# A Mixture-of-Experts and S4 kernel: skip term moved, first two groups re-dealt, S4 paced by single operations

## The chip, the cores and the metric

The kernel runs on one core of one Trainium2 chip. A core has TensorE (PE, matrix products; PEld is its weight load), VectorE (DVE), ScalarE (ACT), GpSimd (POOL) and SyncE (SP), which run their own instruction queues in order and wait for one another by semaphores. SP and POOL issue the DMAs here; those of POOL can add to what lies at their destination. The metric is the time of one execution in microseconds, less is better; several runs are timed, and one execution is recorded by the hardware profiler.

## The reference

One input `u` of 2048 tokens by 512 channels is normalised per token, and the output is the input plus two branches of the normalised `xn`:

```
xn = layernorm(x)
# branch A: S4 convolution, per channel d, along the 2048 tokens
K  = real(sum_n C[d,n] * dt[d] * B[d,n] * exp(dt[d] * A[d,n] * l))
yA = causal_convolution(K, xn) + xn * Dskip
# branch B: 8 experts, all kept (top 8 of 8), so each token goes through each expert
gates = softmax(xn @ w_gate)
yB = sum_e gates[:, e] * (silu(xn @ w1[e]) @ w2[e])        # 512 -> 1792 -> 512
out = x + yA + yB
```

All of it is in 32-bit floats on the outside.

## The kernel before

**Products in halves.** Each operand is split into two 16-bit floats, a high and a low part, and a product is made of three matmuls (high by high, high by low, low by high). ACT makes the high part (a scaled copy), DVE the low part (a scaled subtraction). The scales are powers of two from sums of squares over a weight tensor: ACT squares (`square`, `first_square`), PE totals over the partitions (`pow2_total`), DVE turns the total into an exponent (`pow2_exponent`, `pow2`).

**Tiles.** Tokens go in 4 groups ("token blocks", `tb`) of 512, each 4 tiles of 128. The hidden width 1792 goes in 7 pairs of 256 (`NPR`), taken two at a time by `DQS = [(0, 1), (2, 3), (4, 5), (6,)]`; so a group has four blocks `d`, the last of half the size. The outer order is expert `e`, group `tb`, block `d`; 8 x 4 groups in all.

**A block** (`block`) has four steps, called slots; 16 slots make a group. It uses seven products instead of eight for the first weight (a Strassen-like scheme on sums of operands: `x_sums` makes the seven operands of the tokens, `w1_sums` those of the weights). Products land in three PSUM tiles A, B and C (`hb`), ACT copies A to B and B to C (lines 1337 and after), keeps copies in SBUF (`keep`), POOL adds two of these by DMA, and `activate` applies SiLU and the high split on ACT; the low split follows on DVE later (`flush`). Its result is put on the list `units`. `pop(n)` takes n units off that list and multiplies each with the second weight into one of four PSUM tiles y: six matmuls of 512 columns. When a tile y has all its 14 units, `evacuate` reads it out on ACT to a tile "ye" and a DMA adds it to the DRAM sum `oacc`. The tiles ye and the skip tiles share one tag, "stg", of four buffers.

**The first group** (`plain`, expert 0, group 0) uses ordinary products, because the seven-product operands aren't there yet. It has 14 slots, one per half pair. In its slots the other preparations happen: squares of the second weight, splits of the first (`plain_split`), and the operands of group 1, which `x_turn` transposes through a PSUM bank on PE. That one bank ("s4") is used in turn by transposes, gate products, totals and S4; `take_bank` hands it on, and who takes it first reads out what the last user left.

**The order is written by hand.** The program is emitted in the order in which each engine shall run it. Dictionaries `early`, `mid` and `side` say what is emitted in which slot, before a slot's product, after it, and after its units (`at(n, f)` puts f in slot n of expert 0, counted 16 per group; `put` takes expert, group, block and slot). `slot` runs them, then `work_on(limit)` lets up to `limit` steps of the next expert's weight work through (list `work`: squares, totals, splits), if they are ready.

**S4** runs behind the products: `background` is a generator that is asked for its next piece while a budget lasts. `bg_run` gives it a share of planned PE time less what DVE was given otherwise; each piece says what it costs (`tt_`, the planner's estimate of a DVE operation), and a piece may say that it must wait. S4 goes in 32 chunks of 16 channels: tables (`s4_tables`), kernel generation, transforms on PE, `s4_conv` on DVE, back transform. Every second chunk needs a new basis (`s4_basis`), whose three sine operations on ACT are put on `act_later` and emitted by `run_later`, in the third slot of the two middle blocks. All S4 must be emitted before the last group: `bg_until("s4")` emits the rest there.

**The skip term** `u + xn * Dskip` of token tile i is loaded by `base(i)` on SP, computed by `base_add(i)` on DVE, and added to `oacc` by `base_send(i)` on POOL, in slots 4 to 13 of expert 1's first three groups and expert 2's first.

Of the kernel before, what the change touches and what calls it, by code (L numbers as in the profile page):

```python
# [32 lines left out]
def s4_moe_kernel(  # L33
# [64 lines left out]
    clock = {"slot": 0, "pe": 0.0, "pe0": 0.0, "dve": 0.0, "dve0": 0.0, "left": 0.0}  # L98
# [147 lines left out]
    def x_high(g, a):  # L246
        hi = xs_["hi"] = sb.tile([P, 7, TH], F16, tag="ta", name=f"xh{g}_{a}", bufs=1)
        for src, n0, n in xs_["f"]:
            S.copy(hi[:, n0:n0 + n, :].rearrange("p o d -> p (o d)"), src.rearrange("p o d -> p (o d)"))

# [7 lines left out]
    def x_turn(g, a, q):  # L258
# [17 lines left out]
        else:  # L276
            xs = sb.tile([P, 8, P], F16, tag="hh", name=f"xs{g}_{a}_{q}", bufs=9)
            S.copy(xs[:, :n, :], tp[:, :n, :])
            bank["at"] = now()
# [5 lines left out]
    def xplain(j, rs8):  # L285
# [4 lines left out]
        hlf = hl.rearrange("p a k t -> p a (k t)")  # L290
        S.copy(hlf[:, 0, :], xn)
        V.tensor_tensor(hlf[:, 1, :], xn, hlf[:, 0, :], op=ALU.subtract)
# [5 lines left out]
    def xplain_out(j):  # L298
        dst = xT0.rearrange("p a k t -> p (a k) t")[:, :, j * P:(j + 1) * P]
        if j % 2:  # L300
            V.tensor_copy(dst, xp[j])
        else:
            S.copy(dst, xp[j])
# [123 lines left out]
    def square(e, w, pr, raw):  # L427
        rf = raw.rearrange("p a c -> p (a c)")
        S.activation(rf, rf, AF.Square, accum_out=rows_of(e, w)[:, pr:pr + 1])

# [56 lines left out]
    def piece_end(e, w, n, ready):  # L487
# [15 lines left out]
        def later():  # L503
            return now() > st["at"] + 1 and bank_free()
# [147 lines left out]
    def s4_tables(c):  # L652
# [6 lines left out]
        for st in range(6):  # L659
# [19 lines left out]
            yield 3 * tt_(2 * nn * L) + 0.3 * (st == 0)  # L679
# [69 lines left out]
    def s4_conv(c):  # L749
# [14 lines left out]
        for m in range(NI):  # L764
# [11 lines left out]
            if m in (1, 3, 5, 7, 9, 12, 15):  # L776
# [24 lines left out]

    def tt_(n):

        return n / 960 + 0.14
# [178 lines left out]
    xplain(0, rs8_0)  # L983
    V.tensor_reduce(row2[:, 0:1], rows_of(0, 0)[:, 0:2], axis=AX.X, op=ALU.add)
    keep_busy(8, ident)
    stA = pow2_total(row2[:, 0:1], 1, "a")
    take_bank()
    xplain(1, rs8_0)
# [3 lines left out]
    sq(2)  # L992
    xplain_out(0)
    low0 = first_split(0)
    keep_busy(8, ident)
    xplain(2, rs8_0)
    low0()
    sq(3)
    xplain_out(1)
    keep_busy(8, ident)  # L1000
    xplain(3, rs8_0)
    sq(4)
    xplain_out(2)
    low1 = first_split(1)
    xplain_out(3)
    keep_busy(6, ident)
# [28 lines left out]
    def piece_sums(pr):  # L1035
# [12 lines left out]
    work.extend((w_[0], w_[1], s_[0], w_[2], s_[1], w_[3], s_[2], w_[4], s_[3], w_[5], w_[6], s_[4], s_[5], s_[6]))  # L1048
# [22 lines left out]
    SHARE = 0.96  # L1071
# [13 lines left out]

    def bg_until(key):
# [5 lines left out]
    def run_later():  # L1092
        while act_later and act_later[0][0] <= clock["slot"]:
            act_later.pop(0)[1]()
            s4["sines"] = now()
# [24 lines left out]
    def evacuate(e, i, y):  # L1120
        g = gates_e[e][:, i:i + 1]
        if e < E - 1 or i < NT - TPB:
            t = sb.tile([P, D], F32, tag="stg", name=f"ye{e}_{i}", bufs=4)
            S.activation(t, y, AF.Copy, scale=g)  # L1124
            if e:
# [43 lines left out]
    def activate(e, tb, d, src, fh, th, whole=False):  # L1169
# [4 lines left out]
        sc = scales[e]  # L1174
# [6 lines left out]
        S.activation(ahl[:, 0, :n], fa, AF.Copy, scale=sc[:, 3:4])  # L1181

        def low():
            V.scalar_tensor_tensor(ahl[:, 1, :n], fa, sc[:, 3:4], ahl[:, 0, :n], op0=ALU.mult, op1=ALU.subtract)  # L1184
# [28 lines left out]

    def at(n, f, where=side):
        where.setdefault((0, n // 16, n % 16 // 4, n % 4), []).append(f)
    for n in range(7):
        at(n // 2, lambda n=n: first_square(1, n, second[n], n % 2 == 1))
    at(0, first_scales, mid)
    at(0, third)
    for n in range(4):  # L1220
        at(2 * n + 1, lambda n=n: plain_split(3 + n))
# [4 lines left out]
    at(6, gates_split)  # L1226
    at(4, lambda: norm_sums(1))
    at(7, lambda: x_stats(1))
    at(8, lambda: x_sums(1, 0))
    at(8, lambda: x_high(1, 0))  # L1230
    at(9, lambda: x_low(1, 0))
    at(9, lambda: x_sums(1, 1))
    at(9, less)
    for n, (a, q, where) in enumerate(((0, 0, early), (0, 1, mid), (0, 2, early), (0, 3, mid))):
        at(10 + n // 2, lambda q=q: x_turn(1, 0, q), where)
# [230 lines left out]
```

## Time and profile before

| what | value |
|---|---|
| median of 3 runs | 2415.71 us (2413.98 to 2416.49) |
| the profiled execution, its own time | 2415.3 us |
| its span, first to last instruction | 2413.5 us |
| PE busy | 2354.6 us (98%) |
| VectorE busy | 1955.1 us (81%) |
| ScalarE busy | 1426.2 us (59%) |
| GpSimd busy | 339.2 us (14%) |
| mean granted TensorE clock | 0.993 |

Busy time is the union of an engine's instruction spans. A wait row names the engine, what it wanted to write and the line, then the engine and instruction whose end released it, and then the total, the count and the longest in us. A timeline row has the start, the length of the merged stretch, the instruction, and in brackets how long the engine stood before it and for whom. A row of groups has the count, then the busy time and the mean length in ns of one, and the idle time before them. A row of windows has, for each stretch, the busy us of PE, PEld, DVE, ACT and POOL with their counts, the granted clock, and the DMA share.

### The profile page before, as it was taken

To read this page: it belongs to the slowest core of one execution; us is meant where nothing else is said; L and a number is where in the kernel's file an instruction comes from. 1 tells how busy PE (TensorE), PEld (TensorE's weight loads), DVE (VectorE), ACT (ScalarE), POOL (GpSimd) and SP (SyncE) were. 2 spreads that over 40 slices of the span, in tenths; PEclk is the share of its full clock that TensorE was granted. 3 is DMA by queue.
4 is the path that set the end of the run, shared out by engine and by line. 5 is a ranking of instruction groups with operands and counts; after the bars stand their busy time and mean duration, and the time that the engine had idled before them with its cause. 6 is when DMAs were issued, how large, how long until landed. Compare 5 with 4: busy or idle time off the path is not lost.

```text
span 2413.5 us, 44927 instructions
## 1 busy us (share of the span) xinstructions
PE 2354.6 (98%) x17663; PEld 1564.7 (65%) x17663; DVE 1955.1 (81%) x3836; ACT 1426.2 (59%) x2435; POOL 339.2 (14%) x394
## 2 busy tenths in 40 slices
PE   7789999999999999999999999999999999999999
PEld 4466666666666666666666666666666666666665
DVE  7663588689985999998889799999898799999611
ACT  6477575555646657565675566665575655754443
POOL 0000001211121110111110111111111101111112
PEclk9899999999999999999999999999999999999999
DMA  6466366574664645565465554655555644633356
GB/s 223 144 164 192 74 173 150 132 176 86 175 144 112 133 98 163 108 135 117 106 162 118 120 132 99 160 116 123 122 115 140 143 110 105 165 65 72 76 115 149
DMA packets 264644, 314.41 MB, mean 130 GB/s; under 512 B 124464, under 2 KB 158768, under 8 KB 264112
## 3 DMA queue, kind: packets, MB, share of 16 engines
q1 hardware_dynamic: 208560, 217.93, 29.6%
q0 software_dynamic: 55872, 93.61, 24.5%
q8 instruction: 138, 2.26, 0.4%
q14 instruction: 74, 0.61, 0.1%
HBM read 201.09 MB, written 60.82 MB: 109 GB/s over the span
## 4 chain that ended last, share of the span: by engine, by line
PE 82%; issue 7%; ACT 4%; DVE 3%; DMA 1%; POOL 1%; SPq 0%; DVEq 0%; POOLq 0%; ACTq 0%
PE hb L1162 36%; PE y L1146 14%; PE y L1148 14%; PE y L1147 14%; PE kgen L690 1%; ACT w1s L432 1%; PE yp L791 1%; PE kf L742 1%; PE uf L731 1%; PE hb L1384 1%; PE tp L267 1%; DVE w1s L435 1%; ACT fa L1179 0%; DMA oacc<-ye 0%; ACT ahl L1181 0%
## 5 line engine op out<-in xcount | busy, mean ns | idle before, releaser
L1162 PE MATMUL hb<-xop,w1s 128*128 128x256 f16 x9114 | 1074.9, 273 | 9.1 <-ACT scC L1333 6.8
L1162 PEld LDWEIGHTS <-w1s 128*128 128x128 f16 x9114 | 889.9, 98 | 186.9 <-issue 11.7
L1146 PE MATMUL y<-w2s,ahl 128*128 128x512 f16 x1792 | 680.6, 380 | 10.2 <-ACT ye L1124 10.2
L1148 PE MATMUL y<-w2s,ahl 128*128 128x512 f16 x1792 | 680.9, 380 | 0.0
L1147 PE MATMUL y<-w2s,ahl 128*128 128x512 f16 x1792 | 680.8, 380 | 0.0
L1148 PEld LDWEIGHTS <-ahl 128*128 128x128 f16 x1792 | 175.4, 98 | 212.1 <-issue 0.8
L1306 POOL DMA_DIRECT2D scC<-sE x124 | 111.6, 900 | 1363.6 <-ACT sE L1333 880.2
L1147 PEld LDWEIGHTS <-ahl 128*128 128x128 f16 x1792 | 175.4, 98 | 177.4 <-issue 12.3
L1146 PEld LDWEIGHTS <-ahl 128*128 128x128 f16 x1792 | 175.4, 98 | 165.2 <-issue 0.8
L774 DVE TENSOR_TENSOR s<-s,tm 128x720 f32<-128x720 f32 (+14 forms) x480 | 269.0, 560 | 16.6
L773 DVE TENSOR_TENSOR tm<-v,k 128x720 f32<-128x720 f32 (+14 forms) x480 | 267.7, 558 | 10.9
L1184 DVE SCALAR_TENSOR_TENSOR ahl<-fa,sc,ahl 128x512 f16<-128x512 f32 (+1 forms) x262 | 178.8, 683 | 90.1 <-ACT ahl L1181 90.0
L1179 ACT ACTIVATE fa<-hb,sc 128x512 f32<-128x512 f32 (+1 forms) x252 | 160.0, 635 | 149.7 <-PE hb L1162 141.1
L1344 ACT COPY hb<-hb 128x512 f32<-128x512 f32 x124 | 64.1, 517 | 261.6 <-PE hb L1162 261.6
L1181 ACT ACTIVATE ahl<-fa,sc 128x512 f16<-128x512 f32 (+1 forms) x262 | 175.9, 671 | 8.6
L1306 POOL DMA_DIRECT2D scB<-sE x124 | 107.2, 864 | 421.5 <-ACT scB L1333 291.1
L1184 DVE SCALAR_TENSOR_TENSOR ahl<-scB,sc,ahl 128x512 f16<-128x512 f32 x124 | 84.4, 681 | 100.0 <-ACT ahl L1181 98.6
L1337 ACT COPY hb<-hb 128x512 f32<-128x512 f32 x124 | 64.4, 519 | 167.1 <-PE hb L1162 165.6
L678 DVE TENSOR_TENSOR tb<-ta,tt 128x64 f32<-128x64 f32 (+2 forms) x192 | 132.2, 689 | 6.6
L676 DVE TENSOR_TENSOR ta<-tb,zr 128x64 f32<-128x64 f32 (+2 forms) x192 | 131.3, 684 | 3.4
L1126 POOL DMA_DIRECT2D oacc<-ye x108 | 96.1, 1308 | 259.9 <-ACT ye L1124 257.2
L677 DVE TENSOR_TENSOR tt<-tb,zi 128x64 f32<-128x64 f32 (+2 forms) x192 | 130.5, 680 | 0.0
(256 smaller groups left out, 2399.1 us busy)
## 6 DMA issues: line engine op xcount, KB each, us to landing
xop<-xd SPq DMA_DIRECT2D x210, 256.0 KB, 3.7
pp<-in_w_dram SPq DMA_DIRECT2D x98, 512.0 KB, 4.4
raw<-in_w_dram SPq DMA_DIRECT2D x56, 512.0 KB, 5.1
oacc<-ye POOLq DMA_DIRECT2D x108, 256.0 KB, 6.5
scC<-sE POOLq DMA_DIRECT2D x93, 256.0 KB, 4.2
scB<-sE POOLq DMA_DIRECT2D x93, 256.0 KB, 4.2
raw<-in_w_dram SPq DMA_DIRECT2D x52, 256.0 KB, 4.0
raw<-in_w_dram SPq DMA_DIRECT2D x104, 128.0 KB, 4.1
```

What stands on the lines that cost most here:

```text
L676: V.tensor_tensor(ta, tin, zrv, op=ALU.mult)
L678: V.tensor_tensor(tout, ta, tt, op=ALU.add)
L773: V.tensor_tensor(tm, v3f[:, :, 0:n], kb, op=ALU.mult)
L774: V.tensor_tensor(s3[:, :, m:], s3[:, :, m:], tm, op=ALU.add)
L1146: T.matmul(y, lhs[0], w2s[pr][:, 0, fh, :], start=(c == 0), stop=False)
L1147: T.matmul(y, lhs[0], w2s[pr][:, 1, fh, :], start=False, stop=False)
L1148: T.matmul(y, lhs[1], w2s[pr][:, 0, fh, :], start=False, stop=(c == NF - 1))
L1162: T.matmul(dst[:, q, :], w1s[pr][:, a, wo, k * P:(k + 1) * P], xop[:, xo, b, k, :], start=(first_mm and q == 0 and n == 0), stop=(n == 5), ...
L1179: S.activation(fa, src[:, :n], AF.Silu, scale=w1_unscale(e, d if whole else prs[0]))
L1181: S.activation(ahl[:, 0, :n], fa, AF.Copy, scale=sc[:, 3:4])
L1184: V.scalar_tensor_tensor(ahl[:, 1, :n], fa, sc[:, 3:4], ahl[:, 0, :n], op0=ALU.mult, op1=ALU.subtract)
L1306: nc.gpsimd.dma_start(dst, src, accum_op=ALU.add)
```

## The change

Four things, in one edit:

1. **The skip term** goes to groups 1 and 2 of experts 1 and 2, and there to later slots: two tiles are loaded in slot 7, two in slot 10, added to in 8, 9, 11 and 12, and sent in 11 and 15.
2. **The first two groups of expert 0** are dealt again. At the start, the transposes of a token tile get a function of their own (`xplain_turn`), one tile's cast is issued before the tile before it is transposed, two squares move behind all four tiles, and three of four copies of the transposes go to ACT. The squares of the second weight begin one slot each, the weight splits come three slots ahead of use and not five, the weight sums (`piece_sums`) become ready eight slots later, so that the second weight's splits go first; the first group's gates move from slot 8 and 9 to 13 and 16; the operands of group 1 are made one slot later, and its last four transposes spread over slots 16 to 18. Two units more each are popped early in plain slots 9 to 12, and fewer in group 1.
3. **Units in a short block**: (1, 2, 0, 1) in its four slots become (1, 1, 1, 1).
4. **Pacing**: S4's share is 0.88 and not 0.96, an operation is estimated 0.04 us cheaper, and pieces are dealt out operation by operation where they are long. A second planner's clock for ACT (`at_`, `act_room`) decides whether sines and weight work are emitted in a slot; sines may go into any slot with room. Totals are not started in a slot next to a transpose.

Its core:

```diff
-        hlf = hl.rearrange("p a k t -> p a (k t)")
-        S.copy(hlf[:, 0, :], xn)
-        V.tensor_tensor(hlf[:, 1, :], xn, hlf[:, 0, :], op=ALU.subtract)
+        S.copy(hl[:, 0].rearrange("p k t -> p (k t)"), xn)
+        xp[j] = (xn, hl)
+
+    def xplain_turn(j):
+
+        xn, hl = xp[j]
+        V.tensor_tensor(hl[:, 1].rearrange("p k t -> p (k t)"), xn, hl[:, 0].rearrange("p k t -> p (k t)"), op=ALU.subtract)
...
-            return now() > st["at"] + 1 and bank_free()
+            return now() > st["at"] + 1 and bank_free() and now() + 1 not in turns
...
             V.tensor_tensor(ta, tin, zrv, op=ALU.mult)
+            if st > 2:
+                yield tt_(2 * nn * L)
             V.tensor_tensor(tt, tin[:, ::-1], ziv, op=ALU.mult)
+            if st > 2:
+                yield tt_(2 * nn * L)
...
-            if m in (1, 3, 5, 7, 9, 12, 15):
+            if m < 8 or m in (9, 11, 15):
                 yield cost
...
-        return n / 960 + 0.14
+        return n / 960 + 0.1
...
-                  lambda: clock["slot"] > 2 * pr + 1)
+                  lambda: clock["slot"] > 2 * pr + 9)
...
-    SHARE = 0.96
+    SHARE = 0.88
...
+    def act_room():
+
+        clock["actleft"] = min(clock["actleft"], 2.0) + clock["pe"] - clock["pe1"] - clock["act"] + clock["act0"]
+        clock["pe1"], clock["act0"] = clock["pe"], clock["act"]
+        return clock["actleft"]
...
-            eb = (1, tb) if tb < NB - 1 else (2, 0)
-            put((*eb, 1 + j // 2, j % 2), lambda i=i: base(i))
-            put((*eb, 1 + j // 2, 2 + j % 2), lambda i=i: base_add(i))
-            put((*eb, 1 + (j + 1) // 2, (3, 1)[j % 2]), lambda i=i: base_send(i))
-        put((0, tb, 2, 0), lambda tb=tb: gates_mm(tb))
-        put((0, tb, 2, 1), lambda tb=tb: gates_dve(tb))
+            eb = (1 + tb // 2, 1 + tb % 2)
+            for n, f in ((7, base), (8 + j % 2, base_add), (11, base_send)):
+                n += 3 if j > 1 else 0
+                n += 1 if j > 1 and f is base_send else 0
+                put((*eb, n // 4, n % 4), lambda i=i, f=f: f(i))
...
+    at(13, lambda: gates_mm(0), mid)
+    at(13, take_bank)
+    at(16, lambda: x_turn(1, 1, 0), early)
+    at(16, lambda: pop(2), early)
+    at(16, lambda: x_turn(1, 1, 2), mid)
+    at(17, lambda: x_turn(1, 1, 1), mid)
+    at(18, lambda: x_turn(1, 1, 3), mid)
+    at(16, lambda: gates_dve(0))
...
-        if s == 2 and 0 < d < len(DQS) - 1:
+        if e == 0:
+            work_lows()
+        room = act_room()
+        if room > 1.0:
             run_later()
...
-        work_on(2 if tb == NB - 1 or tb == 0 or e == 0 else 1)
+        if e + tb == 0 or tb == NB - 1:
+            work_on(2 if room > 2 or e + tb == 0 else 1)
+        elif e == 0 and tb == 1:
+            work_on(2)
+        elif room > 1.0:
+            work_on(1 if room < 2.2 or e else 2)
...
-        if last:
-            pops = (1, 2, 0, 1)
+        if e + tb == 1 - e and d < 2:
+            pops = ((1, 1, 1, 0), (2, 2, 1, 2))[d]
+        elif last:
+            pops = (1, 1, 1, 1)
...
-            slot(0, 0, f // 4, f % 4, (0, 0, 0, 0, 0, 0, 0, 0, 2, 2, 3, 3, 3, 3)[f])
+            slot(0, 0, f // 4, f % 4, (0, 0, 0, 0, 0, 0, 0, 0, 2, 4, 5, 4, 3, 2)[f])
```

More of the change, by code (lines that the diff above doesn't have):

```diff
@@ L96, in s4_moe_kernel @@
     uts = {}
-    clock = {"slot": 0, "pe": 0.0, "pe0": 0.0, "dve": 0.0, "dve0": 0.0, "left": 0.0}
+    clock = {"slot": 0, "pe": 0.0, "pe0": 0.0, "dve": 0.0, "dve0": 0.0, "left": 0.0,
+             "act": 0.0, "act0": 0.0, "pe1": 0.0, "actleft": 0.0}
     bank = {"out": None, "at": -1}
@@ L1225, in s4_moe_kernel @@
     at(6, lambda: done.add("w2 scale"))
[L1226 to L1235, printed above, removed]
-    at(11, lambda: x_high(1, 1))
-    at(12, lambda: x_low(1, 1))
-    for n, (q, where) in enumerate(((0, early), (1, mid), (2, early), (3, mid))):
-        at(13 if q < 2 else 16, lambda q=q: x_turn(1, 1, q), where)
+    at(7, lambda: norm_sums(1))
+    at(8, lambda: x_stats(1))
+    at(9, lambda: x_sums(1, 0))
+    at(9, lambda: x_high(1, 0))
+    at(10, lambda: x_low(1, 0))
+    at(10, lambda: x_sums(1, 1))
+    at(10, less)
+    for n, (q, where) in enumerate(((0, early), (1, mid), (2, early), (3, mid))):
+        at(11 + n // 2, lambda q=q: x_turn(1, 0, q), where)
+    at(12, lambda: x_high(1, 1))
+    at(13, lambda: x_low(1, 1))
+    at(11, gates_split)
+    at(13, lambda: gates_mm(0), mid)
[6 more added lines that the diff above has]
+    at(16, lambda: gates_dve(0))
     for tb in range(NB):
```

86 lines of the change are left out of this document (60 added, 26 removed).

## The prediction, on record before the run

> **What bounds the kernel now.** I read the page first: engines, slices, then who waits for whom.
>
> ```profile
> span 2413.5 us, 44927 instructions
> PE 2354.6 (98%) x17663; PEld 1564.7 (65%) x17663; DVE 1955.1 (81%) x3836; ACT 1426.2 (59%) x2435; POOL 339.2 (14%) x394
> ```
>
> TensorE is the bound. Nothing here removes a product, so the change can earn only time in which PE stands still or runs at half rate, and that is early. PE's waits in three stretches (0 to 320 us, 320 to 720, 720 to the end; columns: total, times, longest):
>
> ```profile
> PE tp L267 <- DVE lgs L348: 12.1, 1, 12.1
> PE tp L296 <- ACT xhl L291: 10.3, 4, 6.6
> PE tp L267 <- ACT xs L278: 4.6, 2, 3.5
> PE tp L267 <- ACT st_w L164: 3.8, 2, 3.0
> PE tot_w L166 <- DVE r L390: 2.9, 1, 2.9
> PE hb L1162 <- ACT hb L1337: 2.4, 2, 2.1
> ```
> ```profile
> PE y L1146 <- ACT ye L1124: 10.2, 4, 3.5
> PE hb L1162 <- ACT scC L1333: 1.6, 2, 0.8
> ```
> ```profile
> PE hb L1162 <- ACT scC L1333: 5.2, 6, 1.2
> ```
>
> After 720 us only 5.2 us are left. A wait also has a tail, as PE's timeline shows:
>
> ```profile
> 24.03 3.80 PE L1384 MATMUL hb<-tb,w1s 128*128 128x512 f16 x12
> 27.81 13.11 PE L1384 MATMUL hb<-tb,w1s 128*128 128x512 f16 x60
> 43.85 0.58 PE L166 MATMUL tot_w<-r,ones 128*128 128x1 f32 x2 [2.93 <-DVE r L390]
> 44.30 10.76 PE L1384 MATMUL hb<-tb,w1s 128*128 128x512 f16 x36
> 75.74 0.37 PE L267 MATMUL tp<-ident,xh 128*128 128x128 f16 x2 [12.11 <-DVE lgs L348]
> 76.55 4.85 PE L1384 MATMUL hb<-tb,w1s 128*128 128x512 f16 x12
> ```
>
> Sixty products take 13.11 us (0.218 each). Behind the 2.93 us gap 36 take 10.76 instead of 7.9, so that gap cost 2.9 twice; behind the 12.11 us gap 12 take 4.85 instead of 2.6. I price a tail at 2 to 3 us wherever PE stood 2.9 us or more.
>
> **The change, part by part.**
>
> **A, the skip term.** A group of four token tiles has 16 slots of 4.6 us (the identity product below comes once per group, 30 groups in 2203.9 us). Now the first two skip tiles share the four "stg" buffers with the four read-outs of y in slots 4 and 5. The fourth read-out must wait for the first one's DMA:
>
> ```profile
> L1355 PE MATMUL hb<-xop,ident x31: 272/273/273, 186.0 to 2389.9; 128*128 128x256 f16 x31
> ```
> ```profile
> ACT ye L1124 <- DMA oacc<-ye: 11.5, 4, 3.6
> oacc<-ye POOLq DMA_DIRECT2D x108, 256.0 KB, 6.5
> base<-in_u_dram SPq DMA_DIRECT2D x16, 256.0 KB, 4.8
> ```
>
> PE then waits 10.2 us for ye. With loads in slots 7 and 10, sends in 11 and 15, no skip tile holds a buffer at the read-out, which stays in slot 5 (the pops add up to the same backlog: 20 + 2 + 22 of group 0 and 1, before 16 + 28). What moves with it: 16 loads on SP, which find buffers whose DMAs (6.5 us from the end of slot 5) end about then, 48 DVE operations, 16 adding DMAs on POOL (14% busy, nothing behind them for two slots). A load now lies one slot (4.6) ahead of its first reader and lands in 4.8, so DVE may stand up to a few us; no row after 75 us has PE waiting for DVE, which is the cover. Worth -10.2 and one tail of 2 at best, 0 at worst; I take -11.
>
> **B, one unit in each slot of the short block.** Its second and third slots had 2 and 0 units, now 1 and 1. A unit is six matmuls, 1.3 us. The third slot's wait (1.6 + 5.2 = 6.8, eight times, once per expert) is then covered, but the second loses 1.3 of cover:
>
> ```profile
> 1220.48 0.36 ACT L1344 COPY hb<-hb 128x256 f32<-128x256 f32 x1
> 1221.90 1.47 PE L1162 MATMUL hb<-xop,w1s 128*128 128x256 f16 x12
> 1224.29 0.38 PE L1162 MATMUL hb<-xop,w1s 128*128 128x256 f16 x2 [0.80 <-ACT scC L1333]
> ```
>
> The copy that the product needs ends at 1220.84; with one unit less PE is there at 1220.6 and waits 0.24. Net 0.56 eight times, -4.5 (0 to -6.8).
>
> **C, the start.** The first product starts at 24.03. ScalarE's durations there:
>
> ```profile
> L291 ACT CAST xhl<-xn 128x512 f16<-128x512 f32 x4 | 2.5, 615 | 2.7 <-DVE xn L288 2.7
> L432 ACT ACTIVATE w1s<-raw,sA 128x1024 f16<-128x1024 f32 x2 | 2.3, 1148 | 0.0
> L303 ACT COPY tb<-tp 128x1024 f16<-128x1024 f16 x2 | 2.0, 995 | 0.0
> L962 ACT ACTIVATE w1s<-raw 128x1024 bf16<-128x1024 f32 x2 | 2.1, 1058 | 0.2 <-issue 0.2
> ```
>
> New order from 10.6 (xn0 ready): four casts 2.5, one square with its read-out 1.25, two copies 2.0, a split 1.15, the total's copy 0.16 and gaps of about 0.5 for it bring ACT to 18; the last tile's transposes (PE, behind the idle ones) end near 19.2, its copy near 20.2. First product 3.7 us earlier. But two squares and a split now come after it (2.8 us), so the scales come only about 1 us earlier, the third weight piece (split right behind them) is late for the fifth product by about 1.4, and the w2 total comes at 40.6 instead of 43.85, PE still waiting about 2 for it, which is short of 2.9 and has no tail. PE enters the seventh product at 41.0 instead of 44.3, and without the tail: 6 us ahead. This is inside the sum of D.
>
> **D, up to group 1's first transposes.** PE's 12.1 us wait is VectorE's string:
>
> ```profile
> 28.00:43.00 15.00, 12.92 (x60) 5.65 (x58) 13.79 (x30) 14.19 (x24) 0.00 (x0) 1.00 0.65 224
> 42.00:76.00 34.00, 20.04 (x109) 9.25 (x110) 30.71 (x80) 19.41 (x27) 0.00 (x0) 0.77 0.28 92
> ```
> ```profile
> L435 DVE SCALAR_TENSOR_TENSOR w2s<-raw,sc,w2s 128x1024 f16<-128x1024 f32 x4 | 5.0, 1278 | 0.0
> L1184 DVE SCALAR_TENSOR_TENSOR ahl<-fa,sc,ahl 128x512 f16<-128x512 f32 x4 | 3.0, 746 | 0.0
> ```
>
> The columns of the window rows are the stretch, then PE, PEld, DVE, ACT, POOL. DVE is busy 30.7 of 34 us there, ACT 14.2 of 15 before it. Ahead of the transposes the string loses one weight sum (1.5 with its low half 1.3), the second x_sums (seven operations, 2.7), the gates' sum and split (1.4), and gains three w2 halves (3.8) and one ahl (0.75): 2.4 shorter, and it starts about 1.5 earlier. The transposes come near 72 instead of 75.74. The larger gain is beneath: they move one product later and the read-outs start earlier (11 units before them, not 4), so PE has done 2.6 + 7 x 1.3 = 11.7 us more by then. Lead into group 1: 3.6 + 11.7 = 15.3. PE still stands about 4 us there (72 less some 68) and has its tail. Bounds: 3 if the units wait for w2's halves in turn, 22 if the string hides wholly. The sums' five remaining pieces move into group 1: 5 x 2.8 on DVE, 5 x 1.14 on ACT, beside PE there.
>
> [...]
>
> **E, groups 1 and 2 of expert 0.** Waits for xs, st_w and hb: 4.6 + 3.8 + 2.4 = 10.8, two of them over 3 with a tail of about 2: 15 us. Each is a transpose, total or copy caught behind ACT's squares; the change deals squares only where ACT has room, one transpose step per slot, totals away from transposes. Against it stand the five splits (5.7 us of ACT) and four units less of cover in group 1 (24 against 28). I take half, -7 (+5 to -15).
>
> **F, S4's share, single operations, sines in any slot.** No PE wait after 720 us names DVE, so a gentler S4 frees nothing. The sines:
>
> ```profile
> L634 ACT ACTIVATE zi<-bf x16: 499/534/545, 305.1 to 2140.8; 128x352 f32<-128x352 f32 x16
> ```
>
> Three operations of 0.5 to 0.6, 16 times, now at any place with room: 0 to 0.8 (B's gap, the nearest) each; I take +3 for all new waits of this kind. The budget is the danger, below.
>
> Sum: -11 - 4.5 - 15.3 - 7 + 3 = -35. The profiled execution took 2415.3 (span 2413.5), the median is 2415.71: 2380.
>
> **The rivals.**
>
> **S4 misses its deadline (the other side).** All of S4 must be emitted before the last group; what isn't is put there in one piece, PE standing.
>
> ```profile
> L791 PE MATMUL yp<-z,dftt x128: 378/379/382, 490.8 to 2294.4; 128*128 128x256 f32 x128
> L1290 POOL DMA_DIRECT2D oacc<-ys x16: 822/1262/2167, 2324.6 to 2381.8; - x16
> ```
>
> S4's last product is at 2294.4, the last group's first step at 2324.6: one slot off, 25 us of room, worth 25 x (0.88 - 0.13) = 19 of credit. The share falls by 0.08 of some 2018 us of PE time at the planner's own prices (28 groups of 68.25, 32 chunks of 3.6): -161. The cheaper estimate (0.04 per operation) gives back 61.5 x 32 x 0.04 less 6 = 72 for S4's operations and about 24 for the other 600: short by 161 - 96 - 19 = 46. That must come from time which S4 now loses waiting for sines, issued in only two slots of 16. DVE behind four chunk ends, and behind one without the wait:
>
> ```profile
> 431.80:467.00 35.20, 31.68 (x211) 21.10 (x210) 14.62 (x32) 20.11 (x36) 8.76 (x10) 0.95 0.79 180
> 724.00:762.00 38.00, 38.00 (x262) 25.37 (x261) 13.07 (x31) 25.59 (x45) 6.99 (x8) 1.00 0.62 139
> 1324.00:1347.50 23.50, 23.50 (x161) 15.54 (x160) 11.31 (x28) 16.03 (x29) 5.27 (x6) 1.00 0.79 169
> 1910.00:1933.00 23.00, 23.00 (x158) 15.23 (x156) 10.82 (x26) 14.82 (x27) 5.27 (x6) 1.00 0.79 171
> 659.00:663.00 4.00, 4.00 (x36) 3.30 (x35) 3.93 (x10) 3.05 (x5) 0.86 (x1) 1.00 0.49 141
> ```
>
> DVE idles 20.6 + 24.9 + 12.2 + 12.2 = 70 us. Sines in the next slot with room return most of that, 55 to 70 against the 46 needed: it fits, narrowly. If nothing returned, 46 of credit at real prices (about 1.1) and a dozen hops of PE, ACT and DMA make some 55 to 60 us with PE idle: 2380 + 57 = 2437. It outweighs the gains from 35 us of missing work on.
>
> **The early blocks only trade waits.** DVE and ACT are both near full from 28 to 76 us; moved work may meet them elsewhere. Then A and B stay (-15.5): 2400.
>
> **Everything hides.** D's remaining stand and tail go (-6.5), E in full (-8), F's +3 too, B at -6.8: 2360.
>
> **It does not do what it says:** ACT takes over as the bound in group 1 and sines break into slots; +20 against A, B and the start: 2415.
>
> **How the numbers follow.** Forecast 2380 (own range 2368 to 2392): 0.48. Only trading: 0.22. All hidden: 0.12. S4 late: 0.11. Nothing gained: 0.07. A change within 0.2% (4.8 us) can't be told from none. Faster 0.82, same 0.05, slower 0.13. The range leaves out S4 late and half of "nothing": 2357 to 2408.
>
> **What would show it.** A: no PE wait on ye between 370 and 680. B: no 0.8 us gap behind the identity product once per expert. C: first product near 20. D: the first transposes of group 1 near 72, group 1 reached some 15 us earlier. E: fewer waits for xs and st_w. F: sines about 16 us after their inputs at most, S4's last product before the last group. Wrong it would be if S4's last back-product stood behind a long PE gap at the end, or if new PE waits on ACT came once per group, since 31 groups multiply what four blocks save.

## The result and the profile after

The changed kernel takes 2381.88 us (median of 4 runs, 2380.24 to 2382.27) against 2415.73 us of the kernel before (median of 4, 2413.98 to 2416.49): a ratio of 0.986, with a 95% interval from 0.9843 to 0.9877. It is 34 us faster; 2380 was forecast. The profiled execution took 2381.7 us and has a span of 2379.9 us, 33.6 less than the 2413.5 of before. The differences below are between these two spans.

The heading of the page of the changed kernel and its row of engines:

```profile
span 2379.9 us, 44942 instructions
PE 2345.2 (99%) x17657; PEld 1560.1 (66%) x17657; DVE 1957.3 (82%) x3835; ACT 1421.8 (60%) x2436; POOL 339.4 (14%) x394
```

The matmuls are the same but for six, which only keep PE busy at the start, and VectorE is as busy as before (1957.3 against 1955.1). PE's busy time fell by 9.4 us, most of it half-rate running behind waits that went: by the granted clock such running cost some 12 us behind five waits before and 3.3 behind two after (an estimate, half of the 24.1 and 6.6 us that PE ran in stretches with a granted clock of 0.50). The rest of the 33.6 is time in which PE stood.

PE's waits in the changed kernel, as in the three fences of before, from 0 to 320 us (the four largest, and the one at the second weight's total), 320 to 720, and 720 to the end:

```profile
PE tp L303 <- ACT xhl L293: 7.0, 1, 7.0
PE hb L1189 <- ACT hb L1403: 4.5, 1, 4.5
PE hb L1189 <- ACT scC L1390: 3.3, 2, 2.5
PE tp L269 <- ACT xs L280: 3.2, 5, 0.9
...
PE tot_w L167 <- DVE r L397: 1.7, 1, 1.7
```
```profile
PE hb L1189 <- ACT scC L1390: 0.9, 1, 0.9
```
```profile
PE hb L1189 <- ACT scC L1390: 2.1, 6, 0.5
PE hb L1189 <- ACT hb L1403: 0.4, 1, 0.4
```

The 12.1 us wait for "lgs" and the 10.2 us for "ye" are gone. Two waits of group 1 are new or larger: 4.5 us for the copy "hb" and 2.5 us for "scC". PE's timeline shows the places that the prediction timed: the first product, the total of the second weight with the seventh product behind it, group 1's first transposes and its first product.

```profile
19.21 1.02 PE L1443 MATMUL hb<-tb,w1s 128*128 128x512 f16 x4 [0.65 <-ACT tb L310]
37.43 0.38 PE L167 MATMUL tot_w<-r,ones 128*128 128x1 f32 x2 [1.74 <-DVE r L397]
37.68 9.62 PE L1443 MATMUL hb<-tb,w1s 128*128 128x512 f16 x36
66.56 0.28 PE L269 MATMUL tp<-ident,xh 128*128 128x128 f16 x2
93.95 0.71 PE L1189 MATMUL hb<-xop,w1s 128*128 128x256 f16 x5
```

The same first product of group 1 in the kernel before, and the row of the identity product, which comes once per group, in the changed kernel:

```profile
107.00 0.82 PE L1162 MATMUL hb<-xop,w1s 128*128 128x256 f16 x6
```
```profile
L1414 PE MATMUL hb<-xop,ident x31: 272/273/273, 168.9 to 2356.1; 128*128 128x256 f16 x31
```

With these marks the gain can be followed from the start to the end. By how much the changed kernel is ahead at each:

| mark | before | after | ahead |
|---|---|---|---|
| first product | 24.03 | 19.21 | 4.8 |
| seventh product | 44.30 | 37.68 | 6.6 |
| group 1, first transposes | 75.74 | 66.56 | 9.2 |
| group 1, first product | 107.00 | 93.95 | 13.0, by work done 20.8 |
| identity product, group 1 | 186.0 | 168.9 | 17.1 |
| group 2 | 268.9 | 249.0 | 19.9 |
| group 3 | 338.3 | 318.5 | 19.8 |
| expert 2, group 0 | 713.4 | 681.7 | 31.7 |
| last | 2389.9 | 2356.1 | 33.8 |

At group 1's first product the changed kernel has popped six more units of 1.3 us, so 13.0 + 7.8 = 20.8. (Before that product it pops 22 units and not 16: two more in each of slots 9 and 10, one more in 11, one less in 13, and two in slot 16.) At the identity products it has popped one unit fewer, because the short block now gives its units out evenly; so 1.3 comes off those. The lead is then 20.8 at the start of group 1, 18.5 at group 3, 30.4 at expert 2 and 33.6 at the end of the span. From 320 us on a mark also depends on how many of S4's own products lie before it; the two kernels differ in this by 0.4 to 2.8 us of PE time (an estimate from the counts and the spacing of those matmuls), so these later leads are good to a few us only.

### The profile page after: what moved, and what is told of

It reads as the page before. It is cut to its first block, busy times and chain, and to the rows that moved or that the text cites. A ratio compares the mean times of both kernels' runs of the same rounds, so it can differ in the third digit from the quotient of the medians.

```text
span 2379.9 us, 44942 instructions
## 1 busy us (share of the span) xinstructions
PE 2345.2 (99%) x17657; PEld 1560.1 (66%) x17657; DVE 1957.3 (82%) x3835; ACT 1421.8 (60%) x2436; POOL 339.4 (14%) x394
## 4 chain that ended last, share of the span: by engine, by line
PE 91%; ACT 4%; DMA 2%; DVE 2%; issue 1%; POOL 0%; DVEq 0%; SPq 0%; ACTq 0%; POOLq 0%
PE hb L1189 40%; PE y L1173 15%; PE y L1174 15%; PE y L1175 15%; PE kgen L702 1%; PE kf L754 1%; PE yp L803 1%; PE uf L743 1%; DMA scB<-sE 1%; ACT w1s L440 1%; ACT ahl L1209 0%; ACT fa L1205 0%; PE hb L1443 0%; PE tp L269 0%; DMA oacc<-ye 0%
## 5 line engine op out<-in xcount | busy, mean ns | idle before, releaser
L1361 POOL DMA_DIRECT2D scC<-sE x124 | 118.3, 954 | 1343.8 <-ACT sE L1390 983.8
L786 DVE TENSOR_TENSOR s<-s,tm 128x720 f32<-128x720 f32 (+14 forms) x480 | 268.9, 560 | 16.6
L1218 DVE SCALAR_TENSOR_TENSOR ahl<-scC,sc,ahl 128x512 f16<-128x512 f32 x124 | 84.4, 680 | 58.7 <-ACT ahl L1209 55.5
```

Source lines behind the costliest of these rows:

```text
L786: V.tensor_tensor(s3[:, :, m:], s3[:, :, m:], tm, op=ALU.add)
L1361: nc.gpsimd.dma_start(dst, src, accum_op=ALU.add)
```

## The experiments

The first question was which part pays. Two rivals to the prediction's account were put against it: that S4's pace, named there as a danger, in truth carries the change, and that the many small edits to the order trade one wait for another.

**The skip term alone,** put into the kernel before in its new places:

```diff
-            eb = (1, tb) if tb < NB - 1 else (2, 0)
-            put((*eb, 1 + j // 2, j % 2), lambda i=i: base(i))
...
+            eb = (1 + tb // 2, 1 + tb % 2)
+            for n, f in ((7, base), (8 + j % 2, base_add), (11, base_send)):
...
```

> The kernel before with the skip term alone in its new groups and slots. Theory (buffers at the read-out): the four PE waits on ye (10.2 us) and the slow tail behind one of them vanish, 11 us less than before, about 2404.5. Rival (the waits came from a busy ACT, or the loads only move the wait to VectorE): ye waits stay and the time is within 3 us of before, 2413 to 2416.

Measured: 2420.82 us, a ratio of 1.0023 (1.0013 to 1.0032). It is slower, by about 5 us. The trace shows a gain and a loss. At the first identity product of expert 2 the kernel is 11.8 us ahead of the kernel before, and at group 3 it was 0.5 behind, so it gained 12.3: the four waits for "ye" (10.2 us) and the one tail behind them are gone. Then the lead is lost at one place. PE's waits from 720 us to the end, and the adding DMAs of the last group's first block, of this kernel:

```profile
PE yp L791 <- DVE z L781: 13.9, 1, 13.9
PE hb L1162 <- ACT scC L1334: 5.0, 5, 1.8
```
```profile
L1291 POOL DMA_DIRECT2D oacc<-ys x16: 824/1210/2171, 2334.5 to 2389.7; - x16
```

PE stands 13.9 us for S4's "z" just before the last group, which starts at 2334.5 and not 2324.6. S4's last back product comes at 2329.6 instead of 2294.4: 35 us late, where the kernel before had 25 us to spare. The skip term's 48 VectorE operations are charged to S4's budget, but so they were in the old slots (`base_add` adds the same 2.0 in both), so the charge alone doesn't explain the 35 us. What did grow is S4's waiting for its sines: from the start of a basis's last input on VectorE to its first sine, summed over the sixteen bases, it is 393 us here and 292 in the kernel before; the third basis alone waits 46.1 us and not 3.6. With sines in two slots of sixteen, a basis that is late for one slot waits for the next. Why the move makes bases late was not followed further.

**The skip term and the sines.** The same kernel, with the sines of S4's basis emitted in every slot instead of two of sixteen:

```diff
-        if s == 2 and 0 < d < len(DQS) - 1:
-            run_later()
+        run_later()
```

> The kernel before with two parts: the skip term in its new places, and sines emitted in any slot after they are asked for (no planning of ScalarE's room). Theory: the skip term alone earned 12 us inside and lost 14 to 17 at the last group, because the skip term's VectorE time now came out of S4's budget and S4 was late; with prompt sines S4 is early again, the stand before the last group goes and 12 us are kept, 2403 within 3. Rival (the stand has another cause, or sines in any slot break into PE's work): 2410 or more, with the stand or new waits on ACT in the trace.

Measured: 2406.87 us, 0.9969 (0.9957 to 0.998), some 14 us less than with the skip term alone. The row of S4's back products and PE's two largest waits from 320 us on:

```profile
L791 PE MATMUL yp<-z,dftt x128: 379/379/382, 436.1 to 2204.0; 128*128 128x256 f32 x128
```
```profile
PE hb L1162 <- ACT scC L1333: 7.7, 8, 1.8
PE kf L742 <- DMA kt<-kd: 4.2, 1, 4.2
```

S4 ends at 2204.0, 126 us earlier than with the skip term alone, and no stand is left before the last group. So the stand came from S4's lateness, and the sines cure it; the reason that was expected, a new charge to S4's budget, is not shown, since the charge is the same in both places. By the medians about 9 of the 12 us are kept, a little less than expected. The profiled execution has a new 4.2 us wait of S4's own product for a DMA; but it is the slowest of the six (2411.9 us, the others 2405.7 to 2407.9), so that wait may not be in the others. The waits for "scC" are still there (7.7 in eight): sines in any slot do not cure them.

**Without the sines.** The changed kernel, with sines in the two old slots alone:

```diff
-        if room > 1.0:
+        if s == 2 and 0 < d < len(DQS) - 1:
             run_later()
```

> The changed kernel, but sines are emitted only in the third slot of the two middle blocks, as before; share 0.88. Theory (the sines' wait paid for the share): S4 is late, the rest of it stands ahead of the last group with PE idle, 35 to 65 us slower than the changed kernel, 2417 to 2447. Rival (dealing by single operations paid for it): S4's last back-product still comes before the last group and the time is 2382 within 4.

Measured: 2444.51 us, 1.012 (1.0105 to 1.0136), 62.6 us slower than the changed kernel and slower than the kernel before. PE's waits from 2200 us to the end:

```profile
PE yp L803 <- DVE z L793: 31.4, 2, 19.4
PE kf L754 <- DMA kt<-kd: 9.6, 2, 6.0
PE kgen L702 <- DVE tb L690: 8.4, 1, 8.4
PE yp L803 <- ACT k L757: 6.8, 1, 6.8
```

PE stands 56 us there, hop by hop, while what is left of S4 is emitted in one piece; the last group starts at 2358.0. The rows of the sines and of their last input on VectorE, in the changed kernel, show what the edit does:

```profile
L639 DVE TENSOR_SCALAR bf<-bf x16: 343/344/433, 262.8 to 2049.3; 128x352 f32<-128x352 f32 x16
L642 ACT ACTIVATE zi<-bf x16: 479/496/549, 268.1 to 2055.2; 128x352 f32<-128x352 f32 x16
```

The first sine follows its input by 5.3 us, the last by 5.8, and the longest of the sixteen by 8.2; summed over the sixteen, 86 us. In the kernel before the same sum is 292 us (longest 47.6), and in this experiment 513. So S4's lower share and the sines are one part: at this price the share can't be lowered without them.

**The share alone,** raised to its old value while the cheaper estimate of an operation stays:

```diff
-    SHARE = 0.88
+    SHARE = 0.96
```

> The changed kernel with S4's share at 0.96 again. Theory: no PE wait names VectorE, so the share frees nothing: 2382 within 2, with S4's last back-product some 80 to 100 us earlier (2150 to 2170). Rival (the gentler share keeps VectorE from being late): new PE waits on VectorE or on ahl, 5 us or more slower.

Measured: 2399.16 us, 0.9933 (0.9921 to 0.9946): 17.3 us slower than the changed kernel. "A gentler S4 frees nothing" is wrong. PE's waits from 320 us on in this experiment, and then three waits of ScalarE in it:

```profile
PE hb L1189 <- ACT hb L1395: 7.0, 4, 3.0
PE kgen L702 <- ACT ysb L809: 4.0, 2, 3.7
PE hb L1189 <- ACT hb L1403: 2.8, 3, 1.8
PE hb L1189 <- ACT scC L1390: 2.6, 5, 0.9
```
```profile
ACT w1s L440 <- DVE tw L453: 31.8, 17, 4.6
ACT zi L642 <- DVE bf L639: 13.8, 5, 3.9
ACT uh L731 <- DVE uc L726: 15.6, 10, 3.7
```

The changed kernel has, for the first of these:

```profile
ACT w1s L440 <- DVE tw L453: 3.9, 3, 2.5
```

No wait of PE names VectorE here either, all name ScalarE. But ScalarE in its turn stands 31.8 us for VectorE's sums "tw" and not 3.9, and the PSUM copies that PE waits for are queued behind. PE stands five times for more than 1 us: in ScalarE's timeline three of these copies come behind a split that waited for "tw" (1.5 to 4.5 us) and two behind a sine that waited for its input "bf" (3.8 and 3.9). PE's waits from 320 us on are 13.0 us more than in the changed kernel, and two tails of about 2.9 and 1.7 come with them; that accounts for the 17.3. S4's last back product is at 2051.7, 194 us sooner than in the changed kernel. A queue of VectorE's that is too full reaches PE through ScalarE, and a table of PE's waits doesn't name it.

**The share and the price together** as they were before:

```diff
-        return n / 960 + 0.1
+        return n / 960 + 0.14
...
-    SHARE = 0.88
+    SHARE = 0.96
```

> The changed kernel with both old numbers, share 0.96 and 0.14 us per operation. By the planner S4 then goes 4% faster than at 0.88 with 0.10; at 0.96 with 0.10 it was 13% faster and 17 us slower. Theory (VectorE is given more than it can do, is late, ScalarE waits for it and PE for ScalarE, once per slot that is over-booked): a small part of the 17, 0 to 6 us, 2382 to 2388. Rival (the share itself does it): 2395 or more.

Measured: 2380.06 us, 0.9858 (0.9845 to 0.9872), 1.8 less than the changed kernel, with single times that overlap (2379.05 to 2380.72 against 2380.24 to 2382.27): no difference that these runs can tell. ScalarE's wait for "tw" is 6.1 us in total, PE's for "scC" 1.7 from 320 us on, and S4 ends at 2181.7. Share and price act together, as the rate at which S4 is emitted. Between the old pair and the new there is nothing to choose; the one mixture that was tried hurts.

**The units of the short block** in their old order:

```diff
-            pops = (1, 1, 1, 1)
+            pops = (1, 2, 0, 1)
```

> The changed kernel with units (1, 2, 0, 1) in the short block again. Theory: the 0.8 us gap behind the identity product is back once per expert (6.8 in all) and the smaller gaps before the block's third slot (some 3 us in the changed trace) go: 3 to 4 us more than the changed kernel, about 2385.5. Rival (planning by ACT's room already cured it): no change, 2382 within 1.5.

Measured: 2381.37 us, 0.986 (0.9846 to 0.9873), no difference. PE's waits for "scC" from 320 us on come to 3.6 us in six, against 0.9 + 2.1 = 3.0 (and 0.4 for "hb") with the even order and 6.8 in the kernel before. So what halved them is another part of the change. The sines in every slot are not it (7.7 above), nor share and price (1.7 with the old pair). What is left, above all, is the dealing of ScalarE's work by room (`act_room`) and the finer pieces of S4; neither was tried alone.

**The skip term's slots.** The changed kernel, with the skip term in its new groups but in slots 4 to 13 again:

```diff
             eb = (1 + tb // 2, 1 + tb % 2)
-            for n, f in ((7, base), (8 + j % 2, base_add), (11, base_send)):
...
+            put((*eb, 1 + j // 2, j % 2), lambda i=i: base(i))
+            put((*eb, 1 + j // 2, 2 + j % 2), lambda i=i: base_add(i))
+            put((*eb, 1 + (j + 1) // 2, (3, 1)[j % 2]), lambda i=i: base_send(i))
```

> The changed kernel with the skip term in the new groups but in its old slots (first two tiles loaded in slots 4 and 5, at the read-outs of y). Theory (buffers): the fourth read-out again waits for the first one's DMA, four PE waits on ye of about 2.5 us and a tail or two, 10 to 13 us slower, 2392 to 2395. Rival (the groups mattered, not the slots): 2382 within 3.

Measured: 2400.62 us, 0.9944 (0.9931 to 0.9958), 18.7 us slower than the changed kernel. ScalarE's row from 320 to 900 us, and PE's from 320 to 720 and from 720 on:

```profile
ACT ye L1150 <- DMA oacc<-ye: 14.2, 4, 3.8
```
```profile
PE y L1173 <- ACT ye L1150: 5.6, 2, 2.8
```
```profile
PE y L1173 <- ACT ye L1150: 6.8, 2, 3.4
```

The four waits are back, 12.4 us, with three tails of 1.6 to 1.7. ScalarE waits for the buffers' DMAs, and PE for ScalarE, as the prediction read the four buffers "stg". Some 1.4 us of the 18.7 aren't accounted for by these. S4's last back product comes at 2264.8, 18.9 us later than in the changed kernel, which is as much as the kernel as a whole is later: where the sines are dealt by room, the skip term's slots cost S4 nothing.

**The start.** The changed kernel with the first 24 us in the old order (`xplain` and its transposes in one, squares between the tiles, two copies on VectorE):

```diff
     xplain(0, rs8_0)
-    xplain(1, rs8_0)
     xplain_turn(0)
...
+    xplain(1, rs8_0)
     xplain_turn(1)
...
-        if j == 2:
+        if j % 2:
             V.tensor_copy(dst, xp[j])
```

> The changed kernel with the old order of the first 24 us (each tile cast, subtracted and transposed in turn). Theory: the first product starts near 24 again, but the total of the second weight, which sets when group 1's operands can be made, comes only 1 to 2 us later: 2 to 5 us slower, 2384 to 2387. Rival (only the start of the chain counts): the whole 4.8 us of the first product's shift, 2386.7 or more. Second rival: VectorE's string hides it, 2382 within 1.

Measured: 2388.35 us, 0.9889 (0.9876 to 0.9903), 6.5 slower than the changed kernel. PE's timeline of this experiment:

```profile
24.23 1.03 PE L1444 MATMUL hb<-tb,w1s 128*128 128x512 f16 x2
44.17 0.38 PE L167 MATMUL tot_w<-r,ones 128*128 128x1 f32 x2 [1.74 <-DVE r L397]
44.41 9.62 PE L1444 MATMUL hb<-tb,w1s 128*128 128x512 f16 x36
```

The first product is 5.0 later than with the new order, the seventh 6.7 later, group 1's first transposes 6.7 later (73.3), the first identity product 6.4 later, and the time is 6.5 longer. The rival held: what is lost up to the seventh product is carried on almost whole, and nothing later absorbs it.

**The weight sums early again,** ahead of the second weight's splits (in the list of work the sums stand between the splits, as before):

```diff
-                  lambda: clock["slot"] > 2 * pr + 9)
+                  lambda: clock["slot"] > 2 * pr + 1)
```

> The changed kernel with the weight sums ready eight slots earlier and in the old order among the second weight's splits. Theory (VectorE's string ahead of group 1's transposes): two or three sums of 2.8 us are ahead of them again, the first transposes come 3 to 8 us later than 66.6, and group 1 gains 2 to 4 back because ScalarE has fewer splits there: 0 to 5 us slower. Rival (group 1's crowding outweighs it): faster by 2 or more.

Measured: 2384.98 us, 0.9878 (0.9863 to 0.9893), 3.1 slower than the changed kernel by the medians. The total of the second weight, in PE's timeline:

```profile
43.37 0.59 PE L167 MATMUL tot_w<-r,ones 128*128 128x1 f32 x2 [7.64 <-DVE r L397]
43.82 10.02 PE L1443 MATMUL hb<-tb,w1s 128*128 128x512 f16 x36
```

PE stands 7.64 us there instead of 1.74, and group 1's first transposes come at 73.1 instead of 66.6. By the identity product of group 1 only 3.1 us of these 6.5 remain (171.9 against 168.9): the work that was not pushed into group 1 isn't in the way there. So half of what the later sums gain is paid again within group 1.

**The plain slots' units** as before, (2, 2, 3, 3, 3, 3) from slot 8 on, with (3, 2, 1, 0) and (2, 2, 2, 2) in group 1's first two blocks:

```diff
-            slot(0, 0, f // 4, f % 4, (0, 0, 0, 0, 0, 0, 0, 0, 2, 4, 5, 4, 3, 2)[f])
+            slot(0, 0, f // 4, f % 4, (0, 0, 0, 0, 0, 0, 0, 0, 2, 2, 3, 3, 3, 3)[f])
```

> The changed kernel with the first group's units popped as before (2, 2, 3, 3, 3, 3 from slot 8 on) and four more in group 1. Theory (units fill PE while VectorE's string runs): seven units were popped ahead of the first transposes, now four less, 5.2 us of PE standing there again; group 1 gets them as cover and gives some back: 2 to 5 us slower, 2384 to 2387. Rival (PE had no stand left there): 2382 within 1 or faster, because group 1 stalls less.

Measured: 2384.09 us, 0.9876 (0.9862 to 0.9889), 2.2 slower. PE then stands 2.2 us for "xh" and 4.9 for "xl" at the first transposes, which the early units cover in the changed kernel; some of it comes back in group 1, which has the units instead.

**Pieces only where their data has landed.** The larger of group 1's new waits pointed to one instruction. ScalarE's timeline of the changed kernel, and PE's at the same place:

```profile
121.89 1.06 ACT L436 ACTIVATE pp<-pp 128x1024 f32<-128x1024 f32 x1 [4.45 <-DMA pp<-in_w_dram]
122.86 0.19 ACT L436 ACTIVATION_READ_ACCUMULATOR pp<-pp 128x1 f32 x1
122.95 0.58 ACT L1403 COPY hb<-hb 128x512 f32<-128x512 f32 x1
```
```profile
123.58 0.80 PE L1189 MATMUL hb<-xop,w1s 128*128 128x256 f16 x3 [4.54 <-ACT hb L1403]
```

A square of the next weight was emitted in the slot that issued its load. ScalarE stood 4.45 us for the DMA, and the copy that PE needs stood behind it. The edit lets a piece be emitted only in a later slot than its load:

```diff
-                    it.raw = it.load()
+                    it.raw, it.got = it.load(), now()
...
-        if not it.ready():
+        if not it.ready() or (it.load is not None and getattr(it, "got", -1) >= now()):
             return False
```

> The changed kernel, but a piece of weight work may be emitted only in a slot after the one that issued its load. In the changed trace ScalarE stands 4.5 us at 119 us for a square whose load was issued in the same slot, and PE stands 4.5 behind it, with a slow tail of 1.6. Theory: that wait and its tail go, 5 to 7 us less, 2375 to 2377. Rival (the work is only put off and collides later, or S4 or the weight work gets late): within 2 us of 2382 or slower.

Measured: 2373.51 us, 0.9829 (0.9816 to 0.9843): 8.4 us less than the changed kernel and the fastest kernel of this study. In ScalarE's timeline the square no longer waits, and PE's waits from 90 to 160 us begin with

```profile
PE hb L1189 <- ACT scC L1390: 3.4, 1, 3.4
```

Group 1's first product is at 90.4 us, 3.6 earlier, and the first identity product at 159.6, 9.3 earlier. So 5.7 us come within group 1, close to the wait of 4.54 and its tail of 1.6. The 3.6 before it have a second place of the same kind, a split that waited for its own load. ScalarE's row in the changed kernel:

```profile
68.74 1.15 ACT L440 ACTIVATE w2s<-raw,sc 128x1024 f16<-128x1024 f32 x1 [3.52 <-DMA raw<-in_w_dram]
```

Behind it stood the copy "xop", and PE waited 1.88 us for that copy at 72.2 us. Both waits are gone here. The rest comes ahead of that: the first transposes are 1.5 earlier (65.1).

**Landed pieces, and fewer of them in group 1.** On top of the last edit, two steps per slot only where ScalarE has room:

```diff
-            work_on(2)
+            work_on(2 if room > 2 else 1)
```

> The version with landed loads, and in group 1 of expert 0 two steps of weight work in a slot only where ScalarE has room for more than 2 us, otherwise one. In the trace of landed loads PE stands 3.35 us at 119 us for a copy behind a split and a square of one slot. Theory: that wait goes, 3 to 4 us less than 2373.5, 2369.5 to 2370.5. Rival (the weight sums come late for their blocks, or the squares crowd group 2): 2373 within 1, or slower.

Measured: 2373.56 us, 0.9831 (0.9818 to 0.9845), the same as without it. The wait for "scC" in group 1 stays (3.1 us). But the edit did not reach its place: in both traces the copy "scC" comes behind the same operations on ScalarE, which is busy without a pause for 10 us and more ahead of it. The last two in the version with landed loads are a split and a square; behind them the copy starts at 122.08:

```profile
119.99 1.15 ACT L440 ACTIVATE w1s<-tw,sc 128x1024 f16<-128x1024 f32 x1
121.04 1.05 ACT L436 ACTIVATE pp<-pp 128x1024 f32<-128x1024 f32 x1
```

PE's stand begins at 119.36. So the split and the square fill 2.1 of its 3.35 us, as the theory had it, and an edit that moves them away was not tried.

## Why the prediction was right, and where it was not

The sum came out within 2 us of the time, but not through all of its terms: C and D gained 5.5 us more than predicted and E 9.3 less, and that the two nearly cancel is luck. From the marks, and against the prediction's own:

| term | predicted | measured |
|---|---|---|
| C and D, lead into group 1 | -15.3 | -20.8 |
| E, groups 1 and 2 of expert 0 | -7 | +2.3 |
| A, skip term | -11 | -11.9 |
| B and F, the rest | -4.5 + 3 | -3.2 |
| sum | -35 | -33.6 |

**A was right in its place, and incomplete.** Four waits and a tail, from the buffers: -11.9 in the whole change (about -13, with the last row at about -2, when S4's own products before the mark are counted in), -12.3 alone, and back when only the slots are put back. What the step left out is S4. "No row after 75 us has PE waiting for DVE, which is the cover" was true of the kernel before; with the move alone S4 ends 35 us later and PE stands 13.9 us for VectorE, which turns the gain into a loss of 5. This needs the sines in their two old slots: with sines in every slot the stand is gone, and in the changed kernel the skip term's slots cost S4 nothing. The danger stood in the text, as a matter of share and price only.

**B failed.** The predicted 0.56 us eight times is nothing measurable. The wait was there, but another part of the change had shortened it already. The prediction's own estimate for that part is in F, as a cost.

**C was right.** "PE enters the seventh product at 41.0 instead of 44.3, and without the tail: 6 us ahead": measured 6.6 at its start (7.8 at the end of its 36 products), and 6.5 by putting the old order back. The two pieces are different, though. The first product is 4.8 earlier, not 3.7; the seventh starts 6.6 earlier, at 37.68; and the tail, said to vanish, is there in the profiled execution (36 products in 9.62 us where 7.9 is full rate).

**D had the mechanism and missed the size.** The transposes were put near 72 with 4 us of standing and a tail; they came at 66.56 with 0.36 us of standing. The mis-sized term is VectorE's string: it was called 2.4 shorter and 1.5 earlier, and it is 9.2 earlier in all, of which 6.6 is there at the seventh product already. The upper bound, "22 if the string hides wholly", is close to what happened (20.8). VectorE's string still ends there: in the execution with the old slots PE is 1.9 us earlier at these transposes, and stands 2.13 us for "xl" until 67.04. The early units are not what hides it alone: with the old pops PE stands 4.9 + 2.2 us there, and only 2.2 us of these reach the end.

**E failed.** Half of 15 us was to be gained. The waits named there for "st_w" went and those for "xs" became small (none over 0.9 us), but group 1 got two others, the 4.54 us with its tail and 2.47, and from group 1's first product to group 3's identity product the lead falls by 2.3 (20.8 to 18.5). "The change deals squares only where ACT has room" is not so there: in group 1 of expert 0 the code has `work_on(2)` without a test of room. Nor had the prediction asked whether a square's data would be there. With that mended, in the landed kernel, E comes to 2.3 - 5.7 = -3.4, half of what was predicted. So for E the rival that early work only trades waits was right; C and D speak against it elsewhere.

**F: its sentence fell, and its +3 did not come.** A faster S4 at the new price costs 17.3 us, so the rate matters, through ScalarE. The rate as changed is a little gentler than with the old pair (S4 ends at 2245.9 and not at 2181.7), and the time is the same. So F's edits of share and price gain nothing, though not for the reason given, and the new waits priced at +3 are not there: from 320 us on PE waits 3.4 us for "scC" and "hb", against 6.8 before.

**The rival on S4** was right as a mechanism and in its price: 57 us for S4 late by 46 of credit (planned us of VectorE's time), and 62.6 with the sines in their old slots. The sines' return was put a little low, at 55 to 70 from four chunk ends. With the skip term moved and sines in every slot S4 ends at 2204.0 and not at 2294.4, 90 us earlier; at 0.96 less 0.13, that is 0.83 of credit per us, this is about 75 (an estimate), and less the 46 it leaves 29. The rows of S4's last back products and of the last group's first adding DMA in the changed kernel agree:

```profile
L803 PE MATMUL yp<-z,dftt x128: 379/379/382, 425.9 to 2245.9; 128*128 128x256 f32 x128
L1345 POOL DMA_DIRECT2D oacc<-ys x16: 822/1262/2162, 2291.8 to 2349.3; - x16
```

There are 46 us between the two, 41 beyond one slot, against 25 before: at 0.75 about 31 of credit. "It fits, narrowly" was right, with a little more room than was thought.

**The clock.** The prediction priced a tail wherever PE stood 2.9 us or more, and none below; that bound was its author's estimate from two gaps, and the runs don't bear it out. Behind 1.74 us of standing at the second weight's total the changed kernel has a tail: 36 products take 9.62 us, and the granted clock is 0.50 from 38.06 to 41.47 us. And in the kernel before, the stand of 3.07 us for "ye" at 676.7 us has none: the granted clock is 1.00 from 676 to 683 us, and the 24 products from 678.63 us on take 2.78 us, as long as the 24 at 523.01 us that had no wait before them.

**What stays open:** which part shortened the waits for "scC" after 320 us, why the skip term's move alone makes S4's bases late for their sines, and whether the wait of 3.4 us left in group 1 of the fastest kernel goes when the split and the square ahead of it are moved.

## What to carry to other kernels

An operation moved in time can delay a background stage on one of its engines, and the loss then shows far from the move: the skip term's move gained its 12 us at the read-outs and lost more at the far end, where S4, tied to two slots of sixteen for its sines, missed its deadline. Before work is dealt to an in-order engine, ask whether its data has landed, not only whether the engine has room: a square and a split that waited for their own loads held up copies that PE needed, and mending that took off 8.4 us. And where an engine is said to free nothing because PE never waits for it, look one step back, at whom the engine waits for that PE does wait for.

## What the runs showed of the hardware that was not expected

**The same gap of 1.74 us has a tail or none.** In the kernels after the change PE stands 1.74 or 1.75 us at the second weight's total, for the same instruction, in nine profiled executions. Behind it 36 products take 9.62 us in five of them (the changed kernel, old units, share 0.96, the old start, landed with room) and 7.93 us in the other four (old slots, old pops, old share and price, landed). Two rows, of the execution with the landed pieces:

```profile
37.67 0.38 PE L167 MATMUL tot_w<-r,ones 128*128 128x1 f32 x2 [1.75 <-DVE r L397]
37.91 7.93 PE L1443 MATMUL hb<-tb,w1s 128*128 128x512 f16 x36
```

against 37.68 and 9.62 of the changed kernel, quoted above: the two begin within 0.3 us of each other. So in these runs the length of the gap alone did not set whether a tail followed.

The window rows of the changed kernel, for the stretch with the gap and the next, show the tail in the granted clock (the third figure from the end): 1.00 while PE is busy for 1.68 of 3.42 us, and 0.50 in the 3.41 us behind.

```profile
34.64:38.06 3.42, 1.68 (x9) 0.73 (x8) 2.67 (x7) 3.35 (x6) 0.00 (x0) 1.00 0.21 85
38.06:41.47 3.41, 3.41 (x9) 1.22 (x8) 2.87 (x6) 2.36 (x5) 0.00 (x0) 0.50 0.00 0
```

No run was made to test what decides between the two outcomes; it stays open.

**A tail need not reach the end.** The old slots have no tail there (7.93 us) and reach group 1's transposes 1.9 us earlier (64.6 against 66.6), but then PE stands 2.13 us for VectorE, and group 1's first product comes at 93.8 against 93.95 in the changed kernel.

**The gap of 7.64 us has hardly a longer tail.** With the weight sums early, behind 7.64 us of standing, 36 products take 10.02 us (2.1 over 7.93); behind 1.74 us they take 9.62 (1.7 over).
